# An mLSTM cell and a squared-ReLU FFN on one core: from group 4 on, FFN1 takes two token groups at once

## The chip, the cores and the metric

The kernel runs on one core of one Trainium2 chip. The metric is the device time of one execution in microseconds (us). A core has five engines with queues of their own: PE (TensorE: matmuls, with its weight loads shown apart as PEld), DVE (VectorE), ACT (ScalarE), POOL (GpSimd) and SP, which here only issues DMAs. Each engine takes its instructions in the order of the program and waits for others by semaphores.

## The reference

```python
def _attn_ref(q, k, v, i_gate, f_gate, o_gate):        # (4, 8, 768, 40); gates (4, 8, 768)
    for t in range(S):
        m_new = np.maximum(f_gate[:, :, t] + m, i_gate[:, :, t])
        f_stab = np.exp(f_gate[:, :, t] + m - m_new)
        i_stab = np.exp(i_gate[:, :, t] - m_new)
        m = m_new
        C = f_stab * C + i_stab * outer(vt, kt)         # per batch and head, 40 x 40
        n = f_stab * n + i_stab * kt
        y[:, :, t] = sigmoid(o_gate[:, :, t]) * (C @ qt) / maximum(abs(n . qt), 1)

def reference(...):
    x = attn_out.transpose(0, 2, 1, 3).reshape(B * S, H * D)      # 3072 tokens x 320
    h = np.maximum(x @ w_in, 0.0)                                 # 320 x 2048
    return h * h @ w_out                                          # 2048 x 320
```

The recurrence over time is computed in chunks of 128 tokens: within a chunk as masked attention with decays, between chunks through the state C.

## The kernel before

**Tiles and groups.** The 3072 tokens are 24 tiles s of 128 (six per batch element). Two tiles make a group g, so there are 12 groups; group g is tiles 2g and 2g+1. A tile first goes through attention and leaves its x (128 tokens x 320), then its group goes through FFN1 (320 to 2048, ReLU, square) and FFN2 (2048 back to 320).

**The path of a tile.** `attend_begin` and `attend_end` hold the products of a section: state times q, weights times values, and the new state. Between the two halves stands one tiny DVE operation (L790) that the second half waits for; other products of PE are put there. DVE then transposes the numerators into `tn`, SP stores them to DRAM (`store_num`, L868) and loads them back turned (`load_num`, L873, four DMAs), `normalise_turned` (L885 to L898) makes x, SP stores x (`store_rows`, L926) and loads it back in squares (`load_rows`, L931, four DMAs), and `turn_squares` (L938) finishes the transposition on DVE. k and q come the same way: `load_squares` (L398) on SP's queue after the numerators, then `turn_kq` (L405) on DVE. `scores`, `weigh` (the exponentials on ACT, L509) and `weighted` (the product on DVE, L608) prepare the next section; `mask` and `values` are on POOL, which also issues the loads of k and v and `pair_up`.

**FFN1 from group 2 on.** A 2x2 scheme with seven products in place of eight (Strassen in Winograd's form): the two halves of the first 256 input rows, the even and odd blocks of 128 output features, and the two tiles of the group. `ffn1_open` computes four of the products for a quarter of the features into PSUM tiles X, Y, V, Z, `ffn1_rows` adds the last 64 input rows as 64x64 products, and `ffn1_close` accumulates three more products and combines all with DVE; `ffn1_square` is ReLU and squaring on ACT. Every block product is 128x128 weights against 128 token columns; a group has 56 of them and 64 row products. The differences of x that the scheme needs come from `sums_of_x`, on POOL from group 3 on. One product of the program is two matmuls in the trace.

**FFN2 from group 1 on.** The same scheme with 160 output columns per product, in four steps of `ffn2_fast` (16, 16, 16 and 8 products). `sums` makes the differences of the squared activations S1, S2, S4 on DVE. The order of PE within a group is A11*B11 (X), S2*T1 (Y); A12*B21 onto X, A21*B12 onto Y; S1*T0 (X), A22*T2 (Y); S4*B22 onto X. DVE's additions after each product (L1072) read the PSUM tile into y, and free it for the next.

**The order of the work** is written out by hand: there is no scheduler, and each engine runs what the program lists for it in that order. The last loop goes over 88 parts, alternately the four FFN2 parts of group g and the four FFN1 parts of group g+2, with the steps of a section at fixed parts (attention of tile s = 6 + n//4 at part n). PSUM has five banks for the FFN (`ps_h`) and three for attention. The activations of a group lie in one of three buffers, `g2_0`, `g2_1` and `g2_c`, taken in turn.

Of the kernel before, what the change touches and what calls it, by code (L numbers as in the profile page):

```python
# [9 lines left out]
F32 = mybir.dt.float32  # L10
# [3 lines left out]
AF = mybir.ActivationFunctionType  # L14
ALU = mybir.AluOpType
PSUM = bass.MemoryType.PSUM

P = 128
# [11 lines left out]
def kernel(  # L30
# [27 lines left out]
    nc = tc.nc  # L58
    B, H, S, D = q.shape
    BH = B * H  # L60
    NB = S // P
    NT = B * NB
# [3 lines left out]
    DM = H * D  # L66
    DFF = moe_w_in.shape[1]
    NF = DFF // P
    NPAIR = NF // 2
    GT = 2  # L70
    NG = NT // GT
    W = 4 * P
    WG = GT * P
# [11 lines left out]
    ps_h = banks.enter_context(tc.tile_pool(name="ps_h", bufs=3, space=PSUM))  # L85
# [35 lines left out]
    w_in2 = consts.tile([P, NPAIR, P], F32)  # L121
# [198 lines left out]
    st = {}  # L320

    W_IN = 6
    flat_c = g2c[:].rearrange("p f t -> p (f t)")
# [12 lines left out]
    HALVES = slice(0, DP), slice(DP, 2 * DP)  # L336
# [580 lines left out]

    def xT_half(s):
        g, j = divmod(s, GT)
        if j == 0:  # L920
            st["xT", g] = xts.tile([P, GT, 3, P], F32, name="xT")
        return st["xT", g][:, j]

    def store_rows(s):
        t = st[s]["xT"] = xT_half(s).rearrange("p c t -> p (c t)")
        nc.sync.dma_start(x_d[s].rearrange("c t d -> t c d"), st[s]["x"][:].rearrange("p (c d) -> p c d", c=3))  # L926
# [14 lines left out]
    def turn_rows(s):  # L941
        d = st[s]
        t = xT_half(s)
        tp = ps_at.tile([P, 3, P], F32, name="tp", tag="at")
        for a in range(2):
            nc.tensor.transpose(tp[:, a, :], d["x"][:, a * P : (a + 1) * P], ident[:])
        for rows in HALVES:
            nc.tensor.matmul(
                tp[rows, 2, :], lhsT=d["x"][:, DM - KR : DM], rhs=ident[:], start=True, stop=True, skip_group_check=True,
            )  # L950
        nc.scalar.copy(t, tp[:])
        del st[s]
# [67 lines left out]
    DH = DM // 2  # L1020
    wo = w_out[:].rearrange("p (f two) d -> p f two d", two=2)
    B11, B12 = wo[:, :, 0, :DH], wo[:, :, 0, DH:]
    B21, B22 = wo[:, :, 1, :DH], wo[:, :, 1, DH:]
    T = {}
# [72 lines left out]
            nc.sync.dma_start(out[t * P : (t + 1) * P, :], y0[:])  # L1097


    win4 = [w_in[:, j, :].rearrange("p (n two f) -> p n two f", two=2, f=P) for j in range(2)]  # L1100
    F11, F12 = win4[0][:, :, 0, :], win4[1][:, :, 0, :]
    F21, F22 = win4[0][:, :, 1, :], win4[1][:, :, 1, :]
    WS = {}
# [84 lines left out]
    def ffn1_square():  # L1188
        if "open" in st:
            g4 = st.pop("open")  # L1190
            P0, P1 = slice(0, P), slice(P, 2 * P)
            nc.scalar.activation(g4[:, :, 1, P0], g4[:, :, 1, P0], AF.Relu)
            nc.scalar.activation(g4[:, :, :, P1], g4[:, :, :, P1], AF.Relu)
            nc.scalar.activation(g4[:, :, :, P0], g4[:, :, :, P0], AF.Square)
            nc.scalar.activation(g4[:, :, :, P1], g4[:, :, :, P1], AF.Square)

    def turn_halves():
        for m in range(2):
            for own in range(2):
                x = PR * (m ^ own ^ 1)  # L1200
                nc.scalar.copy(b_R[HALVES[m], :, :, own], b_T[HALVES[1 - own], :, :, x : x + PR])

    def do(f, s):
        if 0 <= s < NT:
            f(s)
# [59 lines left out]
    ffn = ctx.enter_context(tc.tile_pool(name="ffn", bufs=2))  # L1265
# [37 lines left out]
    for u in range(8):  # L1303
        s = 2 + u // 2
# [107 lines left out]
    ps_h = ctx.enter_context(tc.tile_pool(name="ps_h", bufs=5, space=PSUM))  # L1412
# [3 lines left out]
    for t in C_b:  # L1416
        nc.gpsimd.memset(t[:], 0.0)
    parts = []
    for g in range(NG):
        parts += [(2, g, i) for i in range(4)]  # L1420
        if g + 2 < NG:
            parts += [(1, g + 2, i) for i in range(4)]
    ROUNDED = (17, 18)
    assert ROUNDED[-1] == len(pieces)

    for n, (which, g, i) in enumerate(parts):
        s, at = NB + n // 4, n % 4
# [3 lines left out]
        even = s % 2 == 0  # L1431
# [96 lines left out]
        if at == 2:  # L1528
            if n > 2:
                do(lambda s: weigh(s, masked=True), s + 1)  # L1530
            ffn1_square()
            if even:
                do(weighted, s + 1)
            do(normalise_turned, s)
            do(store_rows, s)
            if n == 2:
                pair_up(9)
                turn_squares(5)
                sums_of_x(2)
                load(8)  # L1540
            if not even:
                do(load_A, s + 2)
            if n > 2:
                do(load_o, s + 5)
                do(load_rows, s)
            if s == NB + 1:
                pair_up(s + 3)
# [3 lines left out]
        if even and at == 3 and s > NB:  # L1551
            do(pair_up, s + 3)
            do(pair_up, s + 4)
        if even and at == 3 and s > NB:
            do(load, s + 4)
        if n == 4:
            sums_of_weights(1)
# [4 lines left out]
        if at == 0:  # L1562
            ffn1_square()
        if n < len(ROUNDED):
            while rounding.done < ROUNDED[n]:
                rounding.step()


# [28 lines left out]
```

## Time and profile before

| | |
|---|---|
| median of the runs shown | 484.83 us (483.25 to 486.61, 3 runs) |
| the profiled execution's own time | 486.42 us |
| its span | 484.7 us |
| PE, PEld, DVE, ACT, POOL busy | 476.5, 443.9, 342.4, 243.2, 224.9 us |
| FFN2 products (L1056) | 1232 matmuls of 160 columns |
| FFN1 block products (L1132) | 1120 matmuls of 128 columns |
| FFN1 row products (L1165) | 1280 matmuls, 64x64 weights, 128 columns |

The span runs from the first instruction to the last one's end; the execution's own time is 1.7 us longer. Busy time counts an instruction from its start to its end; matmuls overlap in the pipeline, so their rate is read from start to start and not from their durations. A line of a wait gives who waited for whom, the total in us, how often, and the longest. A line of the timeline gives the start, the time from the first start to the last end, the engine, the line of the program, what is written and read, and how many instructions; in brackets stands idle time before it and what ended that.

### The profile page before, as it was taken

To read this page: it belongs to the slowest core of one execution; us is meant where nothing else is said; L and a number is where in the kernel's file an instruction comes from. 1 tells how busy PE (TensorE), PEld (TensorE's weight loads), DVE (VectorE), ACT (ScalarE), POOL (GpSimd) and SP (SyncE) were. 2 spreads that over 40 slices of the span, in tenths; PEclk is the share of its full clock that TensorE was granted. 3 is DMA by queue.
4 is the path that set the end of the run, shared out by engine and by line. 5 is a ranking of instruction groups with operands and counts; after the bars stand their busy time and mean duration, and the time that the engine had idled before them with its cause. 6 is when DMAs were issued, how large, how long until landed. Compare 5 with 4: busy or idle time off the path is not lost.

```text
span 484.7 us, 15567 instructions
## 1 busy us (share of the span) xinstructions
PE 476.5 (98%) x6307; PEld 443.9 (92%) x6309; DVE 342.4 (71%) x722; ACT 243.2 (50%) x534; POOL 224.9 (46%) x336
## 2 busy tenths in 40 slices
PE   8999999999999999999999999999999999999997
PEld 4886787779999999999999999999999999999997
DVE  7979868798897866767775956857966956635441
ACT  4699799634743723923622931742942741513300
POOL 5464544656598096098097088089083040020000
PEclk9999999999999999999999999999999999999999
DMA  8999998788977776777677758849655612200000
GB/s 174 200 261 248 284 210 207 213 151 201 183 148 197 141 149 177 135 151 178 129 132 197 139 98 223 142 98 225 126 110 143 126 46 84 57 28 3 1 27 28
DMA packets 192696, 69.93 MB, mean 144 GB/s; under 512 B 158128, under 2 KB 181360, under 8 KB 192624
## 3 DMA queue, kind: packets, MB, share of 16 engines
q1 hardware_dynamic: 186400, 58.68, 56.0%
q0 software_dynamic: 6080, 10.16, 8.6%
q8 instruction: 50, 0.82, 0.7%
q14 instruction: 22, 0.18, 0.1%
q10 hardware_dynamic: 144, 0.10, 0.1%
HBM read 55.69 MB, written 18.92 MB: 154 GB/s over the span
## 4 chain that ended last, share of the span: by engine, by line
PE 83%; DMA 5%; DVE 4%; ACT 3%; SPq 2%; issue 1%; POOL 1%; DVEq 0%; POOLq 0%; ACTq 0%
PE h_ps L1056 32%; PE h_ps L1132 24%; PE h_ps L1165 7%; PE h_ps L972 4%; PE h_ps L1010 4%; PE numT L819 3%; PE numT L799 2%; ACT g_c L515 1%; PE numT L830 1%; DMA num_rows<-tn 1%; DMA kqT<-kq_rows 1%; PE h_ps L983 1%; PE tp L594 1%; PE h_ps L586 1%; PE tp L586 1%
## 5 line engine op out<-in xcount | busy, mean ns | idle before, releaser
L478 POOL TENSOR_SCALAR_AFFINE_SELECT A_bc<-A_bc 64x512 f32<-64x512 f32 x32 | 23.1, 721 | 88.1 <-ACT kq L496 59.3
L1146 ACT COPY r_sb<-h_ps 128x512 f32<-128x512 f32 x20 | 11.7, 585 | 84.6 <-PE h_ps L1132 84.6
L1056 PE MATMUL h_ps<-T,S 128*128 128x160 f32 x352 | 51.7, 300 | 0.0
L1056 PEld LDWEIGHTS h_ps<-T,S 128*128 128x128 f32 x352 | 48.9, 190 | 0.4 <-ACT g L1181 0.2
L1056 PE MATMUL h_ps<-w_out,g 128*128 128x160 f32 x336 | 49.2, 303 | 0.0
L1056 PEld LDWEIGHTS h_ps<-w_out,g 128*128 128x128 f32 x336 | 46.1, 190 | 1.3 <-issue 0.9
L1072 DVE TENSOR_TENSOR y_sb<-y_sb,h_ps 128x160 f32<-128x160 f32 x44 | 14.0, 318 | 45.2 <-PE h_ps L1056 45.0
L1132 PE MATMUL h_ps<-xT,w_in 128*128 128x128 f32 x320 | 43.4, 278 | 0.7 <-issue 0.7
L1132 PE MATMUL h_ps<-lent_t,w_in 128*128 128x128 f32 x320 | 42.3, 275 | 0.0
L1132 PEld LDWEIGHTS h_ps<-xT,w_in 128*128 128x128 f32 x320 | 39.2, 192 | 1.6 <-issue 1.2
L1132 PEld LDWEIGHTS h_ps<-lent_t,w_in 128*128 128x128 f32 x320 | 38.9, 192 | 0.8 <-issue 0.8
L375 POOL DMA_DIRECT2D va<-in_v_dram x64 | 39.3, 626 | 0.0
L1165 PE MATMUL h_ps<-xT,w_in 64*64 64x128 f32 x960 | 39.2, 272 | 0.0
L1132 PE MATMUL h_ps<-lent_t 128*128 128x128 f32 x320 | 39.1, 275 | 0.0
L1132 PEld LDWEIGHTS h_ps<-lent_t 128*128 128x128 f32 x320 | 37.3, 192 | 0.2 <-issue 0.2
L509 ACT ACTIVATE A_bc<-A_bc,b_R 128x64 f32<-128x64 f32 (+1 forms) x128 | 35.7, 361 | 1.0 <-POOL A_bc L478 0.6
L1165 PEld LDWEIGHTS h_ps<-xT,w_in 64*64 64x64 f32 x960 | 34.8, 133 | 1.3
L853 DVE STREAM_TRANSPOSE tn<-numT 128x256 f32<-128x256 f32 x36 | 14.0, 428 | 27.9 <-PE numT L799 18.9
L1124 POOL TENSOR_TENSOR lent_t<-xT 128x128 f32<-128x128 f32 (+1 forms) x18 | 15.6, 887 | 32.7 <-DVE xT L938 32.7
L972 PE MATMUL h_ps<-xT,w_in 128*128 128x256 f32 x128 | 30.1, 386 | 0.5 <-POOL w_in L236 0.4
L1056 PE MATMUL h_ps<-w_out,g_c 128*128 128x160 f32 x192 | 28.0, 302 | 0.0
L972 PEld LDWEIGHTS h_ps<-xT,w_in 128*128 128x128 f32 x128 | 23.4, 190 | 5.0 <-POOL w_in L236 1.3
(233 smaller groups left out, 1148.1 us busy)
## 6 DMA issues: line engine op xcount, KB each, us to landing
A_bc<-a_slots SPq DMA_DIRECT2D x32, 256.0 KB, 4.3
kq<-num_rows SPq DMA_DIRECT2D x80, 64.0 KB, 2.2
num_rows<-tn SPq DMA_DIRECT2D x18, 256.0 KB, 2.5
raw<-in_moe_w_out_dram SPq DMA_DIRECT2D x7, 640.0 KB, 5.7
kqT<-kq_rows SPq DMA_DIRECT2D x34, 128.0 KB, 3.8
og<-in_o_gate_dram SPq DMA_DIRECT2D x24, 160.0 KB, 4.9
x_rows<-x_sb SPq DMA_DIRECT2D x20, 192.0 KB, 3.4
xT<-x_rows SPq DMA_DIRECT2D x80, 48.0 KB, 3.3
```

The source lines that it names most:

```text
L375: eng.dma_start(dst[HALVES[n], PR * (1 - late_keys) : PR * (2 - late_keys)], src[HALVES[late_keys], PR * m : PR * (m + 1)],)
L478: nc.gpsimd.affine_select(part, part, compare_op=ALU.is_ge, fill=-1e30, base=0, pattern=[[0, PR], [0, 2], [1, DP]], channel_multiplier=-1,)
L509: nc.scalar.activation(A[0][:, x, to], A[0][:, x, to], AF.Exp, bias=b_R[:, b, c, own, x : x + 1],)
L819: nc.tensor.matmul(d["numT"][m][HALVES[e], i, t0:], lhsT=va_w[s % NKQ][keys, at * D1 : at * D1 + DP], rhs=rhs, start=(s % NB == 0 and i == ...
L853: nc.vector.transpose(to[:, 2 * m : 2 * m + 2], d["numT"][m].rearrange("p c t -> p (c t)"))
L972: nc.tensor.matmul(hs[i][:, n, :], lhsT=w_in[:, a, fb * P : (fb + 1) * P], rhs=xT[:, :, a, :], start=(n == 0 and a == 0), stop=False,)
L1010: nc.tensor.matmul(st["o_ps"][j], lhsT=st["g2", 0][:, fb, j * P : (j + 1) * P], rhs=w_out[:, fb, :], start=(fb == 0), stop=(fb == NF - 1),)
L1056: nc.tensor.matmul(to, lhsT=lhsT[:, p], rhs=rhs[:, p, :], start=(start and p == 0), stop=(p == NPAIR - 1), skip_group_check=True,)
L1072: add = lambda to, a, b: nc.vector.tensor_tensor(to, a, b, op=ALU.add)
L1124: sub = lambda to, a, b: eng.tensor_tensor(to, a, b, op=ALU.subtract)
L1132: nc.tensor.matmul(to[:, n, :], lhsT=lhsT[:, 4 * q + n, :], rhs=rhs, start=(start and n == 0), stop=True, skip_group_check=True,)
L1165: nc.tensor.matmul(to[cols, n, :], lhsT=w_in2[rows, 4 * q + n, cols], rhs=rhs, start=(start and n == 0), stop=True, skip_group_check=True,)
```

## The change

- The written-out loop ends in group 3: the parts go on only to the first half of FFN1 of group 3, and the rest is written as three functions. `section` holds the attention of a tile, `first_products(p)` FFN1 of groups 2p and 2p+1 together, and `second_products(p)` FFN2 of the two groups, one after the other.
- FFN1 of groups 4 to 11 makes the 2x2 scheme over two groups in place of two tiles: every block product has 256 token columns (`wide_open`, `wide_rows`, `wide_close`), the features are taken in quarters of four blocks, and the results go to both groups' activations. The number of products per pair of groups falls from 112 to 56, with twice the columns; of row products from 128 to 64.
- The differences of x (`wide_sums`) lie in `g2_c`, as do the x of groups 6, 7, 10 and 11; the activations alternate between two buffers. The first half of each difference is made on POOL, the second on DVE, right before the wide products.
- Two sections (tiles 4p+4 and 4p+5) lie in FFN1 of pair p, two (4p+6 and 4p+7) in FFN2. Scores are put between `attend_begin` and `attend_end` in FFN2's sections, row products in FFN1's.
- FFN2 from group 2 on uses `ffn2_late`: A11*B11 (X), A22*T2 (V); A12*B21 onto X, S2*T1 (Y); A21*B12 onto Y, S1*T0 (Z); S4*B22 onto Z, in four PSUM banks in place of two and two.

```diff
--- before.py
+++ after.py
@@ -917,7 +917,10 @@
 
     def xT_half(s):
         g, j = divmod(s, GT)
-        if j == 0:
+        if j == 0 and g > 5 and g % 4 > 1:
+            at = 5 * WG + (g % 2) * GT * 3 * P
+            st["xT", g] = flat_c[:, at : at + GT * 3 * P].rearrange("p (j c t) -> p j c t", j=GT, c=3)
+        elif j == 0:
             st["xT", g] = xts.tile([P, GT, 3, P], F32, name="xT")
         return st["xT", g][:, j]
 
@@ -1097,6 +1100,46 @@
             nc.sync.dma_start(out[t * P : (t + 1) * P, :], y0[:])
 
 
+    def ffn2_late(g, step, behind_f1):
+
+        if step == 0:
+            st["y"] = [ffn.tile([P, DM], F32, name="y_sb", bufs=3) for _ in range(2)]
+            st["o2"] = [ps_h.tile([P, W], F32, name="h_ps") for _ in range(2)]
+        elif step < 3:
+            st["o2"].append(ps_h.tile([P, W], F32, name="h_ps"))
+        X, V, Y, Z = [t[:, :DH] for t in (st["o2"] + 3 * st["o2"][:1])[:4]]
+        y1, y0 = st["y"]
+        g4 = st["g2", g][:].rearrange("p (f two) t -> p f two t", two=2)
+        cols = [slice(n * P, (n + 1) * P) for n in range(2)]
+        S1, S2, S4 = st["S"]
+        add = lambda to, a, b: nc.vector.tensor_tensor(to, a, b, op=ALU.add)
+        m1, u12, u22 = y1[:, :DH], y0[:, DH:], y1[:, DH:]
+        if step == 0:
+            product(X, g4[:, :, 0, cols[0]], B11, start=True)
+            nc.scalar.copy(m1, X)
+            product(V, g4[:, :, 1, cols[1]], T[2], start=True)
+        elif step == 1:
+            product(X, g4[:, :, 1, cols[0]], B21)
+            nc.scalar.copy(y0[:, :DH], X)
+            product(Y, S2, T[1], start=True)
+            add(u12, Y, m1)
+        elif step == 2:
+            product(Y, g4[:, :, 0, cols[1]], B12)
+            add(m1, m1, Y)
+            product(Z, S1, T[0], start=True)
+            add(u22, m1, Z)
+            if behind_f1:
+                sums(g + 1, slice(0, NPAIR), (1,))
+            add(m1, m1, V)
+            t = g * GT + 1
+            nc.sync.dma_start(out[t * P : (t + 1) * P, :], y1[:])
+        else:
+            product(Z, S4, B22)
+            add(u12, u12, Z)
+            t = g * GT
+            nc.sync.dma_start(out[t * P : (t + 1) * P, :], y0[:])
+
+
...
@@ -1193,6 +1236,88 @@
             nc.scalar.activation(g4[:, :, :, P1], g4[:, :, :, P1], AF.Relu)
             nc.scalar.activation(g4[:, :, :, P0], g4[:, :, :, P0], AF.Square)
             nc.scalar.activation(g4[:, :, :, P1], g4[:, :, :, P1], AF.Square)
+
+    def pair_of(p):
+        if ("g2", 2 * p) not in st:
+            for i in range(2):
+                st["g2", 2 * p + i] = st["g2", 1 + 2 * i]
+        return [st["xT", 2 * p + i] for i in range(2)]
+
+    wide_xs = flat_c[:, : 5 * WG].rearrange("p (n j t) -> p n j t", n=5, j=GT)
+
+    def wide_sums(p, j, eng):
+        xa, xb = pair_of(p)
+        xs = wide_xs[:, :, j]
+        sub = lambda to, a, b: eng.tensor_tensor(to, a, b, op=ALU.subtract)
+        sub(xs[:, 2, :], xb[:, j, 1, :], xb[:, j, 0, :])
+        eng.tensor_tensor(xs[:, 3, :], xs[:, 2, :], xa[:, j, 0, :], op=ALU.add)
+        sub(xs[:, 0:2, :], xb[:, j, 0:3:2, :], xa[:, j, 0:3:2, :])
+        sub(xs[:, 4, :], xs[:, 3, :], xa[:, j, 1, :])
+
+    def wide_blocks(to, lhsT, rhs, q, start):
+        for n in range(2):
+            nc.tensor.matmul(
+                to[:, n], lhsT=lhsT[:, 2 * q + n, :], rhs=rhs, start=(start and n == 0), stop=True,
+                skip_group_check=True,
+            )
+
+    def wide_open(p, q):
+        xa, xb = pair_of(p)
+        X, Y, V, Z = [ps_h.tile([P, 2, GT, P], F32, name="h_ps") for _ in range(4)]
+        st["f1"] = X, Y, V, Z
+        m1, U2, U4 = [ffn.tile([P, 2, GT, P], F32, name="r_sb", bufs=4) for _ in range(3)]
+        st["U"] = U2, U4
+        wide_blocks(X, F11, xa[:, :, 0, :], q, True)
+        nc.scalar.copy(m1[:], X[:])
+        wide_blocks(Y, WS[1], wide_xs[:, 3], q, True)
+        nc.vector.tensor_tensor(U2[:], Y[:], m1[:], op=ALU.add)
+        wide_blocks(V, WS[0], wide_xs[:, 0], q, True)
+        nc.vector.tensor_tensor(U4[:], V[:], U2[:], op=ALU.add)
+        wide_blocks(Z, F22, wide_xs[:, 4], q, True)
+
+    def wide_rows(p, q):
+        xa, xb = pair_of(p)
+        X, Y, V, Z = st["f1"]
+        lo, hi = HALVES
+        pairs = (
+            ((X, lo, xa[lo, :, 2, :], False), (Y, hi, xb[hi, :, 2, :], True)),
+            ((V, lo, xb[lo, :, 2, :], True), (Z, hi, wide_xs[hi, 1], False)),
+        )
+        for pair in pairs:
+            for n in range(2):
+                for cols in HALVES:
+                    for to, rows, rhs, start in pair:
+                        nc.tensor.matmul(
+                            to[cols, n], lhsT=w_in2[rows, 2 * q + n, cols], rhs=rhs,
+                            start=(start and n == 0), stop=True, skip_group_check=True,
+                        )
+
+    def wide_close(p, q):
+        xa, xb = pair_of(p)
+        (X, Y, V, Z), (U2, U4) = st["f1"], st["U"]
+        ga, gb = [
+            st["g2", 2 * p + i][:, 4 * q : 4 * q + 4, :].rearrange("p (n two) (j t) -> p n two j t", two=2, j=GT)
+            for i in range(2)
+        ]
+        wide_blocks(X, F12, xa[:, :, 1, :], q, False)
+        nc.scalar.activation(ga[:, :, 0], X[:], AF.Relu)
+        wide_blocks(Y, F21, wide_xs[:, 2], q, False)
+        wide_blocks(V, WS[3], xb[:, :, 1, :], q, False)
+        tt = nc.vector.tensor_tensor
+        tt(U2[:], U2[:], Y[:], op=ALU.add)
+        tt(ga[:, :, 1], U2[:], Z[:], op=ALU.subtract)
+        tt(gb[:, :, 1], U4[:], Y[:], op=ALU.add)
+        tt(gb[:, :, 0], U4[:], V[:], op=ALU.add)
+        st["wide"] = [st["g2", 2 * p + i][:, 4 * q : 4 * q + 4, :] for i in range(2)]
+
+    def wide_square():
+        if "wide" in st:
+            ga, gb = st.pop("wide")
+            nc.scalar.activation(ga[:, 0::2], ga[:, 0::2], AF.Square)
+            nc.scalar.activation(ga[:, 1::2], ga[:, 1::2], AF.Relu)
+            nc.scalar.activation(ga[:, 1::2], ga[:, 1::2], AF.Square)
+            nc.scalar.activation(gb, gb, AF.Relu)
+            nc.scalar.activation(gb, gb, AF.Square)
 
     def turn_halves():
         for m in range(2):
@@ -1416,10 +1541,10 @@
     for t in C_b:
         nc.gpsimd.memset(t[:], 0.0)
     parts = []
-    for g in range(NG):
+    for g in range(2):
         parts += [(2, g, i) for i in range(4)]
-        if g + 2 < NG:
-            parts += [(1, g + 2, i) for i in range(4)]
+        parts += [(1, g + 2, i) for i in range(4)]
+    parts.pop()
     ROUNDED = (17, 18)
     assert ROUNDED[-1] == len(pieces)
 
@@ -1551,7 +1676,6 @@
         if even and at == 3 and s > NB:
             do(pair_up, s + 3)
             do(pair_up, s + 4)
-        if even and at == 3 and s > NB:
             do(load, s + 4)
         if n == 4:
             sums_of_weights(1)
@@ -1564,6 +1688,126 @@
         if n < len(ROUNDED):
             while rounding.done < ROUNDED[n]:
                 rounding.step()
+
+
+    def section(s, between=None):
+        do(attend_begin, s)
+        if between:
+            between()
+        do(attend_end, s)
+        do(decays, s + 1)
+        do(mask, s + 1)
+        do(decay_C, s + 1)
+        if s % 2 == 0:
+            do(load, s + 3)
+        do(store_num, s)
+        do(load_num, s)
+        do(load_squares, s + 2)
+        if s % 2 == 0:
+            do(load_A, s + 2)
+
+    def weights(s):
+        if s < NT:
+            weigh(s, masked=True)
+
+    def finish(s):
+        do(normalise_turned, s)
+        do(store_rows, s)
+        if s % 2:
+            do(load_A, s + 2)
+        do(load_o, s + 5)
+        do(load_rows, s)
+
+    def fetch_next(s):
+        do(pair_up, s + 3)
+        do(pair_up, s + 4)
+        do(load, s + 4)
+
+    ALL = slice(0, NPAIR)
+
+    def first_products(p):
+        s = 4 * p + 4
+        wide_open(p, 0)
+        section(s, lambda: wide_rows(p, 0))
+        wide_close(p, 0)
+        do(turn_kq, s + 1)
+        if p == 2:
+            spread_slots(3)
+        wide_open(p, 1)
+        do(scale_q, s + 1)
+        weights(s + 1)
+        wide_square()
+        finish(s)
+        do(scores, s + 1)
+        do(weighted, s + 1)
+        wide_rows(p, 1)
+        wide_close(p, 1)
+        fetch_next(s)
+        wide_open(p, 2)
+        wide_square()
+        section(s + 1, lambda: wide_rows(p, 2))
+        wide_close(p, 2)
+        do(turn_kq, s + 2)
+        do(turn_squares, s)
+        wide_open(p, 3)
+        do(scale_q, s + 2)
+        weights(s + 2)
+        wide_square()
+        finish(s + 1)
+        do(scores, s + 2)
+        do(weighted, s + 2)
+        do(turn_kq, s + 3)
+        wide_rows(p, 3)
+        wide_close(p, 3)
+        wide_square()
+
+    def second_products(p):
+        s, g = 4 * p + 6, 2 * p
+        section(s, lambda: do(lambda s: scores(s, ("h", "h")), s + 1))
+        if p > 1:
+            sums(g, ALL, (1, 2))
+        ffn2_late(g, 0, True)
+        do(scale_q, s + 1)
+        sums(g, ALL, (3, 4))
+        ffn2_late(g, 1, True)
+        weights(s + 1)
+        do(weighted, s + 1)
+        finish(s)
+        do(turn_squares, s - 1)
+        do(turn_kq, s + 2)
+        ffn2_late(g, 2, True)
+        fetch_next(s)
+        section(s + 1, lambda: do(lambda s: scores(s, ("h", "h")), s + 2))
+        ffn2_late(g, 3, True)
+        do(scale_q, s + 2)
+        sums(g + 1, ALL, (2, 3))
+        ffn2_late(g + 1, 0, False)
+        weights(s + 2)
+        do(weighted, s + 2)
+        finish(s + 1)
+        do(turn_squares, s)
+        sums(g + 1, ALL, (4,))
+        ffn2_late(g + 1, 1, False)
+        for r in range(s + 2, min(s + 6, NT)):
+            half_tanh(r)
+        if g + 3 < NG:
+            wide_sums(p + 1, 0, nc.gpsimd)
+        ffn2_late(g + 1, 2, False)
+        ffn2_late(g + 1, 3, False)
+        do(turn_squares, s + 1)
+        if g + 3 < NG:
+            wide_sums(p + 1, 1, nc.vector)
+
+    scores(10)
+    weighted(10)
+    turn_kq(11)
+    ffn1_rows(3, 1, True)
+    ffn1_close(3, 1, True)
+    ffn1_square()
+    second_products(1)
+    for p in range(2, NG // 2):
+        first_products(p)
+        second_products(p)
 
 
 # ---- launch: one core; inputs and outputs as the reference has them ----
```

## The prediction

> **What bounds the kernel now.** I read the page first: busy shares, the clock row and the chain that ended last.
>
> ```profile
> span 484.7 us, 15567 instructions
> PE 476.5 (98%) x6307; PEld 443.9 (92%) x6309; DVE 342.4 (71%) x722; ACT 243.2 (50%) x534; POOL 224.9 (46%) x336
> PEclk9999999999999999999999999999999999999999
> ```
>
> TensorE is busy for 98% of the span, at the full granted clock, and the chain lies on PE for 83% of it. A busy PE need not be a dense one, so next I took the waits, limited to PE from 185 us, where the changed part begins, to the end.
>
> ```profile
> PE h_ps L1132 <- issue: 0.7, 1, 0.7
> PE numT L830 <- DVE kq L790: 0.2, 1, 0.2
> ```
>
> That is all: in 300 us PE waits once for 0.7 us and once for 0.2. With the smaller hesitations of its weight loads I call the whole slack 1.5 us. From there on the kernel is one unbroken stream of matmuls, so two things alone move its end: the start-to-start distance of the matmuls, and new waits on PE. The distances come from the timeline of PE:
>
> ```profile
> 59.77 2.32 PE L972 MATMUL h_ps<-xT,w_in 128*128 128x256 f32 x10
> 268.14 1.06 PE L1132 MATMUL h_ps<-xT,w_in 128*128 128x128 f32 x8
> 459.65 2.34 PE L1056 MATMUL h_ps<-T,S 128*128 128x160 f32 x16
> 461.82 2.34 PE L1056 MATMUL h_ps<-T,g 128*128 128x160 f32 x16
> ```
>
> The second number is first start to last end. Taking away one instruction's own duration (0.275 us at 128 columns, 0.300 at 160, 0.386 at 256, from the groups) leaves count minus one distances: (1.06-0.275)/7 = 0.112 us at 128 columns, 2.04/15 = 0.136 at 160, (2.32-0.386)/9 = 0.215 at 256; a longer stretch of 16 with hiccups gives 0.222. One product of the program is two matmuls in the trace. A full FFN2 group is 112 of them, 15.2 us.
>
> **Part 1: block products of 256 columns.** Groups 4 to 11 had 112 block matmuls each, 896 x 0.112 = 100.4 us. They become 448 of 256 columns: 448 x 0.216 = 96.8. That removes **3.6 us** (0.9 with 0.222, 4.0 with 0.215). The 64x64 row products go from 1024 matmuls of 128 columns to 512 of 256. Four run side by side, four in about 0.11 us now (64 in 1.75 to 1.8 us); the nearest row with 256 columns, L983, starts two half-array matmuls every 0.217 us, so four quarters take as long: no change. The additions on DVE and the squares on ACT keep their element counts (ACT has 16 more, shorter instructions); both lie beside PE.
>
> Weight loads halve, and PEld is busy 92%. The Trainium skill, page "TensorE: Matmul & The Clock Gate", sections "LDWEIGHTS (loading the stationary operand)" and "Back-to-back issue gap", would make much more of that: a 128-column load costs about 107 ns and a warm 256-column matmul about 109, so the wide form would be nearly free and save some 47 us. The trace disagrees: 256 columns take 0.215 us, about twice 128, so here the columns bind and not the loads; the sum goes by the row.
>
> **Part 2: FFN2's products in another order.** Before, each product that adds onto a PSUM tile which DVE must read first stood behind another, independent product. In the new function Y = S2*T1 is directly followed by A21*B12 accumulated onto Y, and DVE's sum u12 must read Y between them. The built order of PE shows nothing in between and a wait on DVE at that matmul. The price is in the tail of the trace, where DVE does this addition:
>
> ```profile
> 459.85 0.32 DVE L1072 TENSOR_TENSOR y_sb<-y_sb,h_ps 128x160 f32<-128x160 f32 x1 [2.83 <-PE h_ps L1056]
> 464.19 0.32 DVE L1072 TENSOR_TENSOR y_sb<-y_sb,h_ps 128x160 f32<-128x160 f32 x1 [0.72 <-PE h_ps L1056]
> ```
>
> The product before ends its stream at 459.65, where the next one starts. The addition runs from 459.85 to 460.17, because the last matmul must drain first. The released weight load starts 0.053 us after a DVE end (L790 to L830) and its matmul 0.09 later: 460.31. So a direct hand-over costs 0.66, say **0.67 us**. It comes in every group from 2 to 11: 10 x 0.67 = **6.7 us**.
>
> Z = S1*T0, then S4*B22 onto Z, is the same hand-over with u22. In the first group of a pair an attention section stands between while there are sections (pairs 1 to 4). It is bare in the second group of all five pairs and in the first of pair 5: 6 x 0.67 = **4.0 us**.
>
> In the second group u12 also stands on DVE's queue behind normalise, a transpose and S4. Counted from the end of that section's products on PE: ACT's copy of X at 4.6, eight exponentials 2.24, the weighting product 1.0 (to 8.1), normalise 2.0, transpose 0.46, S4 1.2, u12 0.32, so PE is released at 12.2. PE gets there after 5 products of 2.18, at 10.9. That is 1.3 instead of 0.67: 4 x 0.6 = **2.4 us** for pairs 1 to 4.
>
> **Part 3: what the sections are moved past.** The round trips through DRAM set what DVE waits for. Tile 23 shows one, on DVE and on SP's queue:
>
> ```profile
> 408.02 0.78 DVE L853 STREAM_TRANSPOSE tn<-numT 128x256 f32<-128x256 f32 x2 [1.92 <-PE numT L819]
> 415.34 0.17 DVE L885 TENSOR_SCALAR dm<-kq 128x8 f32<-128x8 f32 x1 [1.02 <-DMA kq<-num_rows]
> 417.08 0.20 DVE L898 COPY x_sb<-x_sb 128x64 f32<-128x64 f32 x1
> ```
> ```profile
> 408.82 0.34 SPq L868 DMA_DIRECT2D num_rows<-tn  x1
> 410.91 1.74 SPq L873 DMA_DIRECT2D kq<-num_rows  x4
> 417.30 0.38 SPq L926 DMA_DIRECT2D x_rows<-x_sb  x1
> 419.39 1.92 SPq L931 DMA_DIRECT2D xT<-x_rows  x4
> ```
>
> Normalise can begin 7.4 us after the products end, takes 1.95, and storing and loading x takes 6.4 to 8.2 (417.30 to 424.0 here; 365.7 to 373.9 with more traffic). So x is back after 16 to 18 us.
>
> (a) The wide products of pair p+1 need all four tiles, the last attended in the middle of the FFN2 stretch before. PE comes there at 10.9+1.3+4.36+0.67+2.18 = 19.4 us, just after x is back. But the last tile's transpose and the sums of x now follow the last y addition on DVE, instead of standing one section ahead on POOL. From the last matmul: drain 0.30+0.04, addition 0.27, transpose 0.46, two differences 0.22+0.28, release 0.15 = 1.72. Cover: one distance plus the X product, 0.14+0.86. Wait 0.72 x 4 = **2.9 us**.
>
> (b) In the second section of each FFN2 stretch the second half of the attention products waits for the tiny DVE operation L790, which stands behind normalise, a transpose of squares, turn_kq (1.24), three additions and S1. Those end about 16.1 us after the section before, PE is there at 15.4: 0.75 x 4 = **3.0 us** (0 to 4).
>
> (c) Where FFN1 of a pair passes into FFN2, turn_kq waits for the k and q squares, whose DMAs are issued behind the num round trip on SP: 11.6 us after the section, then 1.2 on DVE, against 12.1 on PE: 0.8 x 3 = **2.4 us** (0 to 5).
>
> POOL's DMA issues (8.6 us for the two pairings and a load) and ACT's squares (3.9 us for each quarter, of 7.8 on PE) fit between their neighbours. The four subtractions taken from POOL to DVE are in (a). The start up to 190 us is the same.
>
> **Sum.** Lost: 6.7+4.0+2.4+2.9+3.0+2.4 = 21.4. Gained: 3.6+1.5 = 5.1. Net +16. The profiled execution took 486.4 us (span 484.7), so it would be 502.6; the median of the runs shown, 484.83, lies 1.6 lower: **501 us**.
>
> **Rivals.** *Small loss* (485 to 492): only the bare hand-overs count, 6.7+4.0+2.9 = 13.6 less 5.1, +8.5, and DVE's queue is never late. For it: DVE has 29% idle. Against: normalise is already seen waiting for a DMA at 415.34.
> *Faster*: one mechanism, the weight load. If PE's pace is set by loads in the FFN1 stretches, 256 columns start closer than twice 128. It decides below 0.180 us: 448 x (0.216-0.180) = 16 cancels the loss; at 0.112 the time is about 455. Against it stands the 0.215 of L972, an identical instruction with as many loads per matmul.
> *The round trip becomes the pace* (above 510): each section waits for its own normalise before the next weighting product. If it takes 2 us longer than tile 23, say for the traffic of the middle (76% DMA share at 160 to 200 us against 19% at the end), the first half of each FFN1 stretch loses 1.5, the second half 1.5, and each FFN2 stretch 2: 3x3+4x2 = 17 at most, up to 518.
> *It doesn't do what it says*: PE's built order has the 224 wide products and 256 row products, so that is out.
>
> **Chances.** The forecast (492 to 510) 0.60, small loss 0.16, slower round trip 0.18, within 1% because the hand-overs cost half 0.04, faster 0.02. A measurement of this kernel tells about 1% from no change. Range 490 to 511: the low end is the bare hand-overs at a lower price with all of Part 1, the high end (b), (c) and the queue at twice their size. Faster by over 1%: 0.02, within: 0.05, slower: 0.93.
>
> **What would show it.** The wide matmuls start 0.216 us apart; PE waits of 0.5 to 0.7 us for DVE at the B12 and B22 products, some 16 of them, those in second groups longer; a wait at the first sum of x in four places; L830 held by L790. If PE shows the B12 waits and the total stays below 490, then something that I price at nothing was gained. If waits for DMAs stand behind DVE, it is the third rival. What would make it wrong: distances at 256 columns other than L972's, or a round trip that is much longer or shorter beside the new order.

## The result, and the profile after

The changed kernel takes **519.9 us** (median of 4 runs, 515.1 to 521.9) against 485.3 beside it: ratio 1.070, 95% interval 1.062 to 1.079. The direction was right; 501 us and the range up to 511 were not. Its profiled execution took 521.87 us. First the page, as before: busy shares and clock.

```profile
span 520.2 us, 13600 instructions
PE 486.7 (94%) x5349; PEld 423.7 (81%) x5349; DVE 344.6 (66%) x738; ACT 248.2 (48%) x550; POOL 213.3 (41%) x320
PEclk9999999999999899999998999999999899999999
```

PE is busy only 94% of the longer span, and three slices of the clock row show an 8, where before all were 9. The waits of PE from 150 us to the end (total in us, how often, longest):

```profile
PE h_ps L1059 <- DVE y_sb L1115: 12.2, 16, 2.9
PE numT L830 <- DVE kq L790: 8.6, 6, 1.7
PE h_ps L1259 <- DVE g_c L1253: 3.1, 4, 0.8
PE numT L799 <- DVE C L790: 1.6, 2, 1.1
PE h_ps L586 <- DVE kqT L405: 1.6, 1, 1.6
```

(L1059 is FFN2's products, which wait for DVE's additions L1115; L1259 the wide products, which wait for the sums of x, L1253; L586 the scores; L799 and L830 the attention products behind the tiny operation L790.) Before, this list held some 1 us. Now it holds 29 waits with 27.1 us, and all are waits for DVE. The list counts from the modelled end of the matmul before; the stream also loses the drain, 0.300-0.136 = 0.164 us for each of the FFN's hand-overs. With 29 x 0.164 = 4.8 (a little too much for attention's shorter matmuls) that is 32 us.

The second loss is the clock. These are three stretches of the trace: start:end, length, then the busy us of PE, PEld, DVE, ACT and POOL, each with its number of instructions, then the granted clock (0.50 here), the DMA share and GB/s:

```profile
167.00:173.80 6.80, 6.09 (x57) 5.76 (x58) 1.79 (x7) 4.80 (x8) 1.94 (x4) 0.50 0.51 95
283.10:286.50 3.40, 3.40 (x15) 3.40 (x14) 0.32 (x1) 0.00 (x0) 0.33 (x1) 0.50 1.14 144
412.80:416.20 3.40, 3.40 (x14) 3.40 (x14) 3.37 (x6) 2.15 (x5) 1.83 (x2) 0.50 0.23 82
```

Three times PE runs at half its clock, 13.6 us in all; the work done in them takes twice as long, so they cost about 6.8 us (experiment 8 measures this price). Sum: 32+6.8, less the 3.6 for wide products and the 1.5 of old slack, is 33.7; the spans differ by 35.5. About as much as the rest of 2 us lies in the first matmul after each wait: at FFN2's products it lasts 0.403 us and not 0.299, and the second starts 0.240 after it and not 0.136. Over the 29 waits these longer first matmuls add up to 2.3 us.

### The profile page after: what moved, and what is told of

The parts are those of the page before. It is cut to its first block, busy times and chain, and to the rows that moved or that the text cites. A ratio compares the mean times of both kernels' runs of the same rounds, so it can differ in the third digit from the quotient of the medians.

```text
span 520.2 us, 13600 instructions
## 1 busy us (share of the span) xinstructions
PE 486.7 (94%) x5349; PEld 423.7 (81%) x5349; DVE 344.6 (66%) x738; ACT 248.2 (48%) x550; POOL 213.3 (41%) x320
## 4 chain that ended last, share of the span: by engine, by line
PE 66%; DVE 14%; DMA 8%; issue 4%; SPq 3%; ACT 2%; POOL 2%; DVEq 0%; POOLq 0%
PE h_ps L1059 23%; PE h_ps L1259 17%; PE h_ps L1290 5%; PE h_ps L975 4%; PE h_ps L1013 3%; DMA num_rows<-tn 3%; PE numT L819 2%; PE h_ps L1175 2%; PE numT L799 2%; DVE S L1054 2%; SPq L873 1%; DMA kq<-num_rows 1%; DVE y_sb L1115 1%; DMA kqT<-kq_rows 1%; PE numT L830 1%
## 5 line engine op out<-in xcount | busy, mean ns | idle before, releaser
L1059 PE MATMUL h_ps<-w_out,g 128*128 128x160 f32 x480 | 74.1, 310 | 9.2 <-DVE y_sb L1115 9.2
L1059 PEld LDWEIGHTS h_ps<-w_out,g 128*128 128x128 f32 x480 | 68.9, 196 | 12.2 <-DVE y_sb L1115 11.4
L1059 PE MATMUL h_ps<-T,S 128*128 128x160 f32 x352 | 52.1, 302 | 0.0
L1059 PEld LDWEIGHTS h_ps<-T,S 128*128 128x128 f32 x352 | 49.9, 193 | 0.0
L1259 PE MATMUL h_ps<-g_c,w_in 128*128 128x256 f32 x192 | 48.8, 383 | 0.0
L1115 DVE TENSOR_TENSOR y_sb<-y_sb,h_ps 128x160 f32<-128x160 f32 x40 | 12.6, 316 | 47.5 <-PE h_ps L1059 47.0
L1259 PE MATMUL h_ps<-g_c,lent_t 128*128 128x256 f32 x160 | 38.8, 381 | 3.1 <-DVE g_c L1253 3.1
L1259 PEld LDWEIGHTS h_ps<-g_c,w_in 128*128 128x128 f32 x192 | 35.7, 190 | 7.0 <-issue 2.5
L1259 PEld LDWEIGHTS h_ps<-g_c,lent_t 128*128 128x128 f32 x160 | 30.1, 190 | 8.5 <-issue 4.6
L1059 PE MATMUL h_ps<-w_out,S 128*128 128x160 f32 x176 | 26.7, 305 | 2.5 <-DVE y_sb L1115 2.5
L1059 PEld LDWEIGHTS h_ps<-w_out,S 128*128 128x128 f32 x176 | 24.2, 190 | 4.4 <-DVE y_sb L1115 3.9
L975 PEld LDWEIGHTS h_ps<-xT,w_in 128*128 128x128 f32 x128 | 23.5, 190 | 4.9 <-POOL w_in L236 1.3
L496 ACT ACTIVATE kq<-A_bc 64x256 f32<-64x256 f32 x56 | 20.1, 405 | 15.4 <-DMA A_bc<-a_slots 15.2
```

What stands on the lines that cost most here:

```text
L496: nc.scalar.activation(e[rows, j : j + 2, :], A[rows, i::2, own * P : (own + 1) * P], AF.Exp)
L975: nc.tensor.matmul(hs[i][:, n, :], lhsT=w_in[:, a, fb * P : (fb + 1) * P], rhs=xT[:, :, a, :], start=(n == 0 and a == 0), stop=False,)
L1059: nc.tensor.matmul(to, lhsT=lhsT[:, p], rhs=rhs[:, p, :], start=(start and p == 0), stop=(p == NPAIR - 1), skip_group_check=True,)
L1115: add = lambda to, a, b: nc.vector.tensor_tensor(to, a, b, op=ALU.add)
L1259: nc.tensor.matmul(to[:, n], lhsT=lhsT[:, 2 * q + n, :], rhs=rhs, start=(start and n == 0), stop=True, skip_group_check=True,)
```

## The experiments

Diffs are against the changed kernel, or, where it says so, against the kernel before. Kernels of one group ran on one chip beside the kernel before, so the ratios to it are what is compared.

**1. FFN2's order alone, in the kernel before** (before_order). Groups 2 to 11 use the new FFN2, everything else is the old schedule.

```diff
         else:
-            ffn2_fast(g, i)
+            (ffn2_fast if g == 1 else lambda g, i: ffn2_late(g, i, g + 1 < NG))(g, i)
```

> The kernel before with one part of the change alone: FFN2 of groups 2 to 11 in the late order of products, in the old schedule and with FFN1 as before. Theory: 10 hand-overs at the B12 product and 10 at the B22 product, 0.58 to 0.67 us each, none made longer by DVE's queue: +12 to +13 us, 497 to 499, at the full granted clock. Rival (the hand-overs are hidden by the weight loads that PE pulls ahead, and what costs in the changed kernel is the late DVE queue): 485 to 489.

Measured: 498.45 us, ratio 1.028 (1.023 to 1.032), at the full clock. PE's waits from 165 us:

```profile
PE h_ps L1056 <- DVE y_sb L1112: 9.0, 20, 0.5
```

Twenty waits, 9.0 us, with 20 x 0.164 = 3.3 of drain 12.3, and with 0.104 for each longer first matmul 14.4; the times differ by 13.7. A bare hand-over so costs 13.7/20 = 0.69 us, close to the 0.67 of the prediction, and the rival, in which the weight loads hide it, is out.

**2. The same order mended, in the changed kernel** (covered). S1*T0 goes between the two products on Y, and u22 is made in two additions, so that Z is read early.

```diff
-            product(Y, g4[:, :, 0, cols[1]], B12)
-            add(m1, m1, Y)
             product(Z, S1, T[0], start=True)
             add(u22, m1, Z)
+            product(Y, g4[:, :, 0, cols[1]], B12)
+            add(m1, m1, Y)
+            add(u22, u22, Y)
```

> The changed kernel with FFN2's late order mended: S1*T0 stands before A21*B12, so that an independent product lies behind each sum that DVE must read first; one more addition on DVE per group. Theory (each bare hand-over from PE to DVE and back is paid in full): the waits of PE at the B12 and B22 products, 14.8 us in the changed kernel's profile, shrink to 1 to 2 us, left in second groups where DVE is late behind normalise, and the half-clock stretch behind the longest of them goes: 502 to 506 us. Rival (the round trips through DRAM set the pace): the same time is waited at the sums of x and before the attention products; 514 to 520.

Measured: 509.87 us, ratio 1.051 (1.047 to 1.055): 10 us gained, not 14 to 18. The waits of PE from 150 us:

```profile
PE numT L830 <- DVE kq L790: 8.5, 6, 1.6
PE h_ps L1260 <- DVE g_c L1254: 4.0, 4, 1.5
PE numT L799 <- DVE C L790: 2.8, 2, 1.4
PE h_ps L586 <- DVE kqT L405: 2.5, 3, 1.7
```

All sixteen waits at FFN2's products are gone, 12.2 us and their drains. Part came back: the sums of x (L1260 here), L790 in its second row and turn_kq were waited for longer, 3.0 us more than in the changed kernel in the last three rows, and there were five stretches of half clock, 17 us in place of 13.6. The one behind the longest hand-over went, as expected, but each of these five stands behind a wait for L790 of 1.4 us or more.

**3. DVE's order around L790** (dve_order). The four combinations of a pair's last quarter, and S1 of the second group, go behind L790 on DVE's queue. `combine` is what `wide_close(p, 3)` now returns, its four DVE operations; the squares of that quarter on ACT move with them.

```diff
-    def second_products(p):
+    def second_products(p, combine=None):
         s, g = 4 * p + 6, 2 * p
-        section(s, lambda: do(lambda s: scores(s, ("h", "h")), s + 1))
+        def between():
+            if combine:
+                combine()
+                wide_square()
+            do(lambda s: scores(s, ("h", "h")), s + 1)
+        section(s, between)
...
-        ffn2_late(g, 2, True)
+        ffn2_late(g, 2, s + 1 >= NT)
...
-        section(s + 1, lambda: do(lambda s: scores(s, ("h", "h")), s + 2))
+        def with_sums():
+            if s + 1 < NT:
+                sums(g + 1, ALL, (1,))
+            do(lambda s: scores(s, ("h", "h")), s + 2)
+        section(s + 1, with_sums)
```

> The changed kernel with two groups of DVE work moved behind the tiny operation L790: the four combinations of the last quarter of a pair (pairs 2 to 4), and S1 of the second group (pairs 1 to 4). Theory (DVE's queue order holds the second half of the attention products): the waits L586 to L830 of 1.7 to 1.9 us in first sections and of 1.4 us in second ones fall to 0.3 or less; 3 x 1.6 + 3 x 1.2 + 0.6 = 9 us and the half-clock stretch at 412 us: 508 to 512. Rival (the work that is moved is itself late, so PE waits for it a few products further on): 516 to 521.

Measured: 517.68 us, ratio 1.066 (1.062 to 1.071), which the interval of the changed kernel overlaps. The rival was nearer. From 185 us on the waits for L790 fell from 8.6 (7.0 and 1.6) to 0.7, but others took their place:

```profile
PE h_ps L1059 <- DVE y_sb L1115: 12.2, 15, 2.9
PE h_ps L1259 <- DVE g_c L1253: 3.1, 4, 0.8
PE h_ps L1059 <- ACT y_sb L1119: 1.3, 3, 0.4
PE h_ps L1059 <- DVE g L1309: 1.2, 3, 0.6
PE h_ps L586 <- DVE kqT L405: 0.5, 2, 0.3
```

In the same stretch L1115 held 11.7 before, and the three last rows are new. An order that frees one consumer of DVE delays the next; the half-clock time stayed at 13.6 us. So waiting for L790 is shown to come from its place in DVE's queue, but taking it away alone did not bring the time back.

**4. Both edits** (both).

> The changed kernel with both earlier edits: FFN2's products reordered so that no sum is read directly between two products, and the DVE work moved behind L790. Theory (DVE's queue is the second cost: work that is moved behind one wait is waited for at the next one as long as hand-overs stand there; without them it has room): the two gains add up or do better, 10 us from the first and 3 to 6 from the second, and fewer stretches of half clock: 502 to 507. Rival (DVE is simply out of time between FFN1 and FFN2, whatever the order): 508 to 511, as with the first edit alone.

Measured: 505.14 us, ratio 1.044 (1.041 to 1.047), as the theory had it: 4.7 us under the first edit alone, 3.3 by the ratios. Three stretches of half clock are left, 10.2 us in place of 17. PE's first rows from 150 us:

```profile
PE h_ps L1260 <- DVE g_c L1254: 6.5, 4, 3.0
PE h_ps L586 <- DVE kqT L405: 2.8, 3, 1.0
PE numT L830 <- DVE kq L790: 2.1, 3, 1.6
```

What is late now are the sums of the last tile's x, and behind them a transfer:

```profile
285.12 0.32 DVE L1115 TENSOR_TENSOR y_sb<-y_sb,h_ps 128x160 f32<-128x160 f32 x1 [1.39 <-PE h_ps L1059]
285.70 0.58 DVE L941 STREAM_TRANSPOSE g_c<-g_c 128x384 f32<-128x384 f32 x1 [0.26 <-DMA g_c<-x_rows]
```

**5. The sums of x earlier on DVE** (x_early). On top of both edits.

```diff
-        ffn2_late(g + 1, 3, False)
         do(turn_squares, s + 1)
         if g + 3 < NG:
             wide_sums(p + 1, 1, nc.vector)
+        ffn2_late(g + 1, 3, False)
```

> The kernel with both edits (505.14 us) and, besides, the last tile's transpose and the sums of x put before the last y addition on DVE's queue instead of after it. Theory (with the hand-overs gone the round trip of x through DRAM is what is late: DVE waits for the DMA of x in the profile of the kernel with both edits): little changes, 503 to 506, with waits for the DMA in place of waits for DVE. Rival (DVE's order is what is late there, as in the changed kernel): the four waits of 0.8 to 3.0 us fall by 0.5 to 0.8 each and the half clock stretch behind the longest goes: 500 to 502.

Measured: 508.46 us beside 487.82 on that chip, ratio 1.043 (1.035 to 1.050), the same as experiment 4. Times the 484.04 us of the kernel before in experiment 4 it is 505 us, inside what was expected. DVE waits for the transfer of x, also as expected (the view goes from 180 us on):

```profile
DVE xT L941 <- DMA xT<-x_rows: 6.1, 2, 3.1
```

With the hand-overs gone the round trip through DRAM is what arrives last in this place. I found no version that beats the kernel before. What is left of the loss in experiment 4 is of the same kind: 19 waits of PE with 14.9 us from 150 us on, their drains, and some 5 us for the half clock.

**6. Columns** (split): each wide block product as two of 128 columns.

```diff
         for n in range(2):
-            nc.tensor.matmul(
-                to[:, n], lhsT=lhsT[:, 2 * q + n, :], rhs=rhs, start=(start and n == 0), stop=True,
-                skip_group_check=True,
-            )
+            for j in range(GT):
+                nc.tensor.matmul(
+                    to[:, n, j], lhsT=lhsT[:, 2 * q + n, :], rhs=rhs[:, j], start=(start and n == j == 0), stop=True,
+                    skip_group_check=True,
+                )
```

> The changed kernel with each block product of 256 columns made as two of 128, one for each tile; everything else stays. Theory (columns set the pace; wide is worth 8 ns of each pair of matmuls at most): between 2 and 4 us slower than the changed kernel's 519.9, so 521 to 524, start-to-start 0.112 us. Rival (the wide products themselves cost something, for instance at the change from quarter-array products back to full ones): 516 to 519.

Measured: 519.61 us, ratio 1.073 (1.069 to 1.077) beside 1.070 (1.062 to 1.079): no difference. The matmuls are as priced; the timeline of the changed kernel's last pair, where no attention is near, has

```profile
459.93 1.89 PE L1259 MATMUL h_ps<-g_c,lent_t 128*128 128x256 f32 x8
```

so (1.89-0.38)/7 = 0.216 us a matmul, and a whole quarter of a pair takes 8.13 (456.37 to 464.50) against 8.30 before (half of the 16.61 from 434.24 to 450.85, two quarters of one group's FFN1 for each quarter of a pair). But PE's waits from 150 us are 23.9 us in the split kernel against 27.1, and its half-clock time is 10.2 us against 13.6: what the wide form saves in matmuls was waited for again.

**7. The clock: fillers in the changed kernel** (fill).

```diff
+    def fill(to, n):        # n matmuls of bf16 zeros, 512 columns, into a bank that is overwritten later
...
         elif step == 2:
+            if not behind_f1 and g + 1 < NG - 2:
+                fill(st["o2"][3], 8)
             product(Y, g4[:, :, 0, cols[1]], B12)
```

with six more behind the scores of each first section, and before them in pair 1.

> The changed kernel with idle matmuls (512 columns of bf16 zeros, 0.21 us each, into a PSUM bank whose contents are not used) in its longest waits: 8 before the B12 product in second groups 3, 5 and 7, 6 behind the scores in the first FFN2 section of pairs 1 to 4, 6 more before them in pair 1. The waits themselves stay. Theory (the halved granted clock is the price of the gaps): the clock stays at full speed, 5 to 7 us are gained: 513 to 515. Rival (the clock falls for another reason, or the halved clock costs nothing): 518 to 522 with the same halved stretches.

Measured: 518.04 us, ratio 1.068 (1.064 to 1.073). The clock was full from 40 us on in the profile, and 1.000 on average in the other three runs, but the time fell by 1.9 us, not by 5 to 7. The fillers cost time themselves: 54 of 0.21 us are 11 us, and PE's waits from 150 us fell only from 27.1 to 17.1. So this leaves the price open. It has to be measured where the waits are made to measure.

**8. Gaps made to measure** (gap1, gap2, gap2_fill), on top of experiment 1: between two readings of Y, DVE repeats S4 once or twice and u12 once, with the same results. In the third kernel 13 idle matmuls stand in each gap.

```diff
             product(Y, S2, T[1], start=True)
             add(u12, Y, m1)
+            for _ in range(2):                        # gap1: range(1)
+                sums(g, slice(0, NPAIR), (4,))
+            add(u12, Y, m1)
...
         elif step == 2:
+            fill(st["o2"][3], 13)                     # gap2_fill alone
```

> The kernel before with the late order of FFN2 (498.45 us) and the hand-over at the B12 product made longer on purpose in groups 2 to 11: between two readings of Y, DVE computes S4 once more and u12 once more, with the same results, so PE waits about 1.4 us longer ten times. Theory (a gap costs its length, and a half-clock stretch of 3.4 us costs 1.7 more; gaps of 1.9 us alone in dense work don't bring one): 512 to 514 at the full clock. Rival (a gap of 1.5 us is enough to halve the clock): up to ten stretches and 17 us more, 520 to 530.

> The same with S4 computed twice more, so the ten waits are some 2.6 us longer than in the kernel with the late order alone, 3.1 us as the profile shows gaps. Theory: ten such gaps are long enough that about half or all of them bring a stretch of half clock of 3.4 us, 1.7 us each: 525 without any, 533 to 543 with five to ten. Rival (the clock falls only where attention's small products surround the gap): 523 to 527 at the full clock.

> The kernel with the ten long gaps (544.48 us) and 13 idle matmuls (0.21 us each, 2.8 us) in each of them, into a PSUM bank whose contents are overwritten later; the sums that make the wait stay. Theory (halved clock costs half of its stretch, and comes from idle PE): full clock, so 498.45 plus ten times 2.7 and no more: 525 to 528, 17 to 20 us less with more work on PE. Rival (the time over the sum of the gaps has another cause, for instance DVE's additional work delaying something else): 540 to 546 whatever the clock shows.

Measured: 519.87 us (515.7 to 523.1) with ten gaps of 1.85, 544.48 (541.1 to 545.6) with ten of 3.1 to 3.5, and 528.48 (525.3 to 529.4) with those filled. The theory for the short gaps, no stretch and 512 to 514 us, was wrong; the long gaps came out just above their 533 to 543. The last ran on another chip: ratio 1.081 (1.072 to 1.090) against 1.124 (1.119 to 1.129). One such gap in the timeline of the long form, and the clock around it:

```profile
255.15 2.34 PE L1056 MATMUL h_ps<-T,S 128*128 128x160 f32 x16
261.02 4.63 PE L1056 MATMUL h_ps<-w_out,g 128*128 128x160 f32 x16 [3.53 <-DVE y_sb L1112]
265.44 2.83 PE L1056 MATMUL h_ps<-T,S 128*128 128x160 f32 x16
```
```profile
252.00:257.00 5.00, 5.00 (x86) 1.00 0.16 56
257.00:260.00 3.00, 0.49 (x4) 0.94 0.83 182
260.00:267.00 7.00, 5.98 (x24) 0.54 0.90 176
267.00:272.00 5.00, 4.58 (x36) 1.00 0.54 144
```

The same product takes 2.34 us ahead of the gap and 4.63 behind it, and the clock column (the third from the right) falls to 0.54 and is full again after 267. Filled, with PE's fillers in the place of idle time, the clock stays at 1.00 and the whole is some 20 us shorter by the ratios, with 130 matmuls more. So the halved clock follows idle PE, and its cost is shown. In gap1 it differs from run to run: the profiled run (515.66) had two stretches of 3.4 us, and 498.45 + 10 x 1.36 + 2 x 1.7 = 515.5 accounts for it; runs at mean clocks of 0.984 and 0.977 took 522.4 and 523.1. A mean of 0.977 over 521.4 us is 24 us at half clock, or by estimate seven stretches. Gaps of 1.85 us are enough, some of the time.

## Why the prediction was wrong

Point by point, with each group of waits as lost start-to-start time:

| step | predicted | profile after |
|---|---|---|
| wide products (Part 1) | -3.6 | 0.216 us a matmul as priced; 0.7 per pair over a whole stretch, 2.8 |
| u12 hand-overs (Part 2) | 6.7 + 2.4 | 11.3: five first groups 0.65 each, second groups 0.64 to 3.04 |
| u22 hand-overs | 4.0 | 3.5: six of 0.58 |
| sums of x (a) | 2.9 | 3.8: four of 0.95 |
| L790 in second sections (b) | 3.0 | 4.8 |
| turn_kq before the scores (c) | 2.4 | 1.8, but in pair 1; none in pairs 2 to 4 |
| L790 in first sections | none | 7.1: four of 1.7 to 1.9 |
| half clock | none | about 6.8 |
| longer first matmul after a wait | 0.09 in each 0.67 | 2.3 in 29 waits |

**The mechanism held.** PE was one unbroken stream, and the new order put DVE between its products; experiment 1 shows the bare hand-overs (twenty at 0.67 are 13.4 us, measured 13.7). The estimate that the prediction draws from the Trainium skill, page "TensorE: Matmul & The Clock Gate", sections "LDWEIGHTS (loading the stationary operand)" and "Back-to-back issue gap", has the change save some 47 us. The trace stayed with the columns, 0.216 us for 256. Two small slips of the prediction change nothing here: its trace has the weight load and the matmul of L830 only 0.002 us apart, and the 0.09 shows as the longer first matmul instead; and its small loss of 8.5 us makes 493, not 492 or less.

**The first step that failed is the wait for L790 in (b) and (c), which for first sections was put at nothing and cost 7.1 us.** In (b) I had seen that L790 stands behind other work on DVE's queue, and looked for it only in the second section of each FFN2 stretch. In the first section I asked when the scores find turn_kq done, (c), and not when the products after the scores find L790 done. There DVE must first end the four combinations of FFN1's last quarter:

```profile
327.77 1.25 DVE L405 STREAM_TRANSPOSE kqT<-kqT 128x1024 f32<-128x1024 f32 x1 [0.30 <-DMA kqT<-kq_rows]
...
330.83 0.68 DVE L1310 TENSOR_TENSOR g<-r_sb,h_ps 128x512 f32<-128x512 f32 x1
331.54 0.16 DVE L790 TENSOR_SCALAR kq<-numT 1x1 f32<-1x1 f32 x1
```

```profile
329.09 0.98 PE L586 MATMUL h_ps<-kqT 40*64 40x128 f32 x32
331.75 0.44 PE L830 MATMUL numT<-vw,kq 64*64 64x41 f32 x16 [1.68 <-DVE kq L790]
```

The scores started at 329.09 without a wait, and PE stood until 331.75. The prediction's own numbers held this: by (c) turn_kq ends at 11.6+1.2 = 12.8, PE's scores then take some 0.9, to 13.7, and four combinations on DVE, 2.5 us in the timeline of before, last until 15.3. That is 1.6 us of waiting, and experiment 3 shows that it goes when the combinations stand behind L790. In second sections, where (b) looked, the wait cost 4.8 and not 3.0.

**The second is the clock, which the sum did not hold at all.** I took the full clock of the profile before for granted although I forecast some 20 us of gaps. With its 6.8 us and the 7.1 of the first sections, 501 becomes 515, the fastest run of the changed kernel (515.1); the median is 5 us further on.

**The third is a size.** The extra wait of second groups was worked out with x's and the numerators' round trips as in tile 23, where SP's queue is empty. In pair 2 the numerators' store was issued at 270.62, two us after their transposition, behind four loads of x and a store of y on SP's queue, and DVE had to wait for their return:

```profile
277.96 0.17 DVE L885 TENSOR_SCALAR dm<-kq 128x8 f32<-128x8 f32 x1 [1.13 <-DMA kq<-num_rows]
```

That is 10.1 us after the section's products, where the prediction had 8.1. (Weighting had waited 1.5 us for POOL before, but was done at 276.83, so it was not what held DVE.) So u12 was read at 281.4 and the wait was 3.04, not 1.3. This was the third rival's mechanism, at one place; experiments 4 and 5 show DVE waiting for the loads of x in the same way once the hand-overs are gone.

The wide form brought nothing measurable: splitting it again cost nothing, since PE then waited less for DVE (experiment 6).

## What to carry to other kernels

When one engine is an unbroken stream, find for every accumulation which other engine must read the bank between two products, and keep an independent product between them: without it each costs the drain, the read and the release, some 0.7 us here (13.7 us for twenty), though DVE was busy for only 68% of that kernel's span. Walk an in-order queue once for every instruction that PE waits for, the one-element ones too. Where a change opens gaps in a dense matmul stream, add the clock: half of each half-clock stretch, on top of the gap.

## What the hardware showed that was not expected

The granted clock of TensorE halves for 3.4 us, or 6.8, after gaps that are shorter than I had expected: ten gaps of 1.85 us in otherwise dense matmuls brought two stretches in the profiled run, ten of 3.1 to 3.5 brought nine with 41 us together. The Trainium skill, page "TensorE: Matmul & The Clock Gate", section "What's actually happening", has a window of 3413 ns that runs freely, and half rate after an idle one. The traces agree with the window: a stretch lasts one or two of it, and in the changed kernel's profile the second and third stretch begin 34.0 and 72.0 windows after the first (167.02, 283.07 and 412.78 us). They differ in that a window need not be idle as a whole.

Which gap is hit is a matter of where the windows fall, and the trace shows it. From one start of a matmul to the next, 1.7 us at 410.0 brought a stretch and 1.9 us at 329.9 did not. The first gap lies inside the window from 409.37 to 412.78, in which PE was idle for 44%; the second is cut by the end of a window at 330.86, which leaves 23% and 26%. The idle share is not the whole rule: 47% in the window from 197.74 brought no stretch, and in gap1 four windows with 54% brought two.
